# Batch 1's x in two groups of 48 rows, its stage A in side-by-side products, and the last evacuation of stage D a step later

## Chip, core and metric

The kernel runs on one core of one Trainium2 chip. The metric is the device time of one execution in microseconds (us), the median of several runs. Inputs are drawn once and are the same for all kernels.

## What is computed

A two-dimensional Fourier transform of x (8 batches of 3072 rows of 256 numbers), of which the real part is kept, and on its result a channel mix: each row is blended with the row before it, multiplied by weights, squared behind a relu, multiplied again and gated.

```python
def _attn_ref(x):                       # x: (8, 3072, 256)
    X = np.fft.fft(x, axis=1)
    X = np.fft.fft(X, axis=2)
    return X.real.astype(np.float32)

def _moe_ref(x, mu_k, mu_r, w_k, w_v, w_r):
    x_prev = np.concatenate([np.zeros((B, 1, D)), x[:, :-1, :]], axis=1)
    xk = mu_k * x + (1.0 - mu_k) * x_prev
    xr = mu_r * x + (1.0 - mu_r) * x_prev
    k = np.maximum(xk @ w_k, 0.0)       # w_k: 256 x 1024
    v = k * k @ w_v                     # w_v: 1024 x 256
    r = 1.0 / (1.0 + np.exp(-(xr @ w_r)))
    return r * v
```

## The kernel before

**Two halves that overlap.** The transform of a batch runs in stages A, D and C, all of them products on TensorE with tables of sines, each followed by an evacuation from PSUM by ScalarE or VectorE. The channel mix of a batch runs in chunks of 512 rows, six to a batch: products with w_k (`k_piece`, L912), a relu on ScalarE (L922), a square on VectorE (L932), products with w_v (L953; in the first chunks L965), products with w_r (`r_item`, L939) with a sigmoid on ScalarE (L944), and the output's product r·v on VectorE (`v_out`, L975), which is then stored.

**Steps.** A loop over 192 steps and a few more gives the order. Step s does the quarter s % 4 of chunk s // 4's w_k products. Around them stands what a table of `at(step, ...)` and `event(step, ...)` puts there: first the items of kind "x" (`r_item`, stage A by `a_sum` and `a_item`, stage D by `d_item`, the turning product `turned`), then the w_v products, then the events, then the items of kind "w", which are VectorE's (`fold`, `butterfly`, `mix`, `diff`) and the loads, then the output products `v_out` (ahead of the "w" items where the step is listed in `OUT_FIRST`), and last the square. So batch b's transform is computed while batch b−1 is mixed. The order of instructions on each engine is pinned to the order in which the code issues them: an engine that waits holds up all that is queued behind it.

**Batch 1 around steps 8 to 18.** x arrives by GpSimd's queue in two halves h, each as a forward part `xp` (`load_p`, a plain transfer, L138 or L135) and a mirrored part `xm` (`load_m`, a gather by row numbers, L141). `fold` (L172, L174) adds the two into `p`. In batches 0 and 1 the data lie on 96 partitions, one row number each. From batch 2 on they lie on 112 partitions, in two groups of 48 at partitions 0 and 64, each transferred by itself. Stage A of batch 1's half h = 0 is `a_sum` at steps 11 and 12 (L681): 8 products of 96 rows and 208 columns each. It takes `p` as it is. Half h = 1 is `a_item` at steps 13 and 14 (L594, L591): 7 products of 104 columns and 2 of 52 each, on `eo`, which `butterfly` (L211) makes of `p`. The other way of stage A, `a_half` (L663) with `a_slots_0` (L653), is used for batch 2: 48-row products of 52 columns, those of the rows 0 to 47 and those of the rows 64 to 111 in turn, into different PSUM banks. Its tables `w_h` and `w_h0` are made by `half_tables` at step 3 (L535).

Stage D is four `d_item`s (L703): two at step 15, two at step 16, evacuated by ScalarE and VectorE in turn. `turned` at step 17 (L752) then multiplies one column of all 13 units with a table, evacuated by ScalarE. Stage C (`c_pairs`, L803) begins at step 18.

**PSUM.** `ps_w` hands out three buffers of two banks in turn, `ps_v` two of one bank. A product into a buffer waits until the buffer's last contents were read.

## Time and profile before

| | us |
|---|---|
| median of 3 runs | 425.98 |
| lowest and highest | 425.94, 426.00 |
| the profiled execution's own time | 426.17 |
| its span in the profile | 424.4 |
| TensorE busy | 418.4 (99%) |
| VectorE busy | 371.3 (87%) |
| ScalarE busy | 332.4 (78%) |
| GpSimd busy | 64.2 (15%) |

The profile is of one execution. Engines: PE is TensorE's matmuls, PEld its weight loads, DVE VectorE, ACT ScalarE, POOL GpSimd, SP SyncE. L912 is line 912 of the kernel. A row of a timeline gives the start and the time in us, the engine, the line, the operation, the tiles (written <- read), the shape, and the count of merged instructions; in brackets stands an idle time before it and what ended it. A row of the windows gives the stretch, its length, the busy time of PE, PEld, DVE, ACT and POOL with the number of instructions, the granted clock, the share of the transfer engines and GB/s. The granted clock of TensorE is 1.00 throughout the profiled span. Times in the texts below are counted from the span's start.

### The profile page before, as it was taken

The numbers are of one execution on the slowest core, as the hardware profiler recorded it, in microseconds if no ns is written. First come the engines' busy times: TensorE is split into PE (matmuls) and PEld (weight loads), VectorE is DVE, ScalarE is ACT, GpSimd is POOL, SyncE is SP. The second block draws the span as 40 slices with busy tenths as digits, with TensorE's granted clock in tenths as the row PEclk, the third lists the DMA queues.
The fourth block names the chain that finished last, engine by engine and source line by source line (L and its number), as shares of the span: only waits on it lengthen the run. The fifth ranks groups of instructions, "written<-read, shape, count | busy, mean of one in ns | idle before, by whom it ended". The sixth has DMA issues, their size and how long they took to land.

```text
span 424.4 us, 9646 instructions
## 1 busy us (share of the span) xinstructions
PE 418.4 (99%) x3974; PEld 294.1 (69%) x3974; DVE 371.3 (87%) x593; ACT 332.4 (78%) x438; POOL 64.2 (15%) x99
## 2 busy tenths in 40 slices
PE   8999999999999999999999999999999999999996
PEld 3767766776677767776767776777777776776765
DVE  8899999999898999989999899989999676977553
ACT  7889886798768986699767996689876997666661
POOL 7478500200060001400041000500000000000000
PEclk9999999999999999999999999999999999999999
DMA  8779962632385223932349232772233232332333
GB/s 171 111 111 195 224 156 57 113 91 64 70 151 147 64 59 62 215 101 51 76 77 220 52 75 59 134 174 55 52 76 72 58 73 52 74 74 51 76 76 99
DMA packets 35104, 42.08 MB, mean 99 GB/s; under 512 B 4114, under 2 KB 31092, under 8 KB 35060
## 3 DMA queue, kind: packets, MB, share of 16 engines
q1 hardware_dynamic: 27488, 25.41, 24.4%
q0 software_dynamic: 7264, 15.80, 21.8%
q8 instruction: 31, 0.51, 0.5%
q10 hardware_dynamic: 308, 0.26, 0.2%
q14 instruction: 13, 0.11, 0.1%
HBM read 32.08 MB, written 25.17 MB: 135 GB/s over the span
## 4 chain that ended last, share of the span: by engine, by line
PE 98%; DVE 1%; issue 0%; POOL 0%; ACT 0%; POOLq 0%
PE psW L912 39%; PE psV L953 37%; PE psW L939 10%; PE psV L965 3%; PE psW L611 3%; PE psW L235 1%; PE psV L611 1%; PE psW L681 1%; PE psW L703 1%; PE psV L378 1%; PE psW L771 0%; PE psW L803 0%; DVE rw L308 0%; PE psV L703 0%; PE psW L663 0%
## 5 line engine op out<-in xcount | busy, mean ns | idle before, releaser
L922 ACT ACTIVATE rl<-psW 128x1024 f16<-128x1024 f32 x192 | 194.3, 1039 | 79.2 <-PE psW L912 75.5
L912 PE MATMUL psW<-x,wk 128*128 128x512 f16 (+1 forms) x776 | 194.4, 377 | 0.3 <-DVE x L1049 0.3
L953 PE MATMUL psV<-wv_sb,k 128*128 128x256 f16 x1424 | 184.2, 273 | 0.0
L953 PEld LDWEIGHTS <-k 128*128 128x128 f16 x1424 | 136.8, 98 | 38.9
L932 DVE TENSOR_TENSOR k<-rl 128x2048 f16<-128x2048 f16 (+1 forms) x100 | 115.5, 1156 | 32.9 <-ACT rl L922 32.8
L912 PEld LDWEIGHTS <-wk 128*128 128x128 f16 x776 | 75.7, 98 | 53.7 <-issue 0.4
L975 DVE SCALAR_TENSOR_TENSOR o<-psV,r 128x512 f32<-128x512 f32 (+1 forms) x97 | 65.7, 680 | 10.0 <-PE psV L953 9.0
L877 DVE TENSOR_TENSOR x<-y,t 128x1536 f16<-128x1536 f16 (+3 forms) x76 | 62.4, 827 | 2.2
L944 ACT ACTIVATE r<-psW 128x1024 f16<-128x1024 f32 x48 | 50.0, 1043 | 0.8 <-PE psW L939 0.8
L939 PE MATMUL psW<-wr,x 128*128 128x256 f16 x384 | 49.8, 273 | 0.0
L939 PEld LDWEIGHTS <-x 128*128 128x128 f16 x384 | 37.5, 98 | 14.1
L574 ACT ACTIVATE a<-psW 128x832 f16<-128x832 f32 (+4 forms) x36 | 29.0, 851 | 0.2 <-PE psW L663 0.2
L574 ACT ACTIVATE g_all<-psW 128x512 f16<-128x512 f32 (+5 forms) x47 | 26.7, 646 | 0.3 <-PE psW L703 0.2
L494 POOL IOTA gate<- 1x1 int32 x7 | 0.8, 121 | 163.4 <-DVE gate L493 163.4
L141 POOL DMA_INDIRECT xm<-in_x_dram,idx_g x18 | 23.3, 1294 | 5.5 <-issue 5.5
L866 DVE TENSOR_SCALAR t<-d,muf_t 128x1536 f16<-128x1536 f16 (+3 forms) x44 | 21.9, 508 | 0.1
L172 DVE TENSOR_TENSOR p<-xp,xm 112x2304 f16<-112x2304 f16 (+6 forms) x19 | 21.6, 1139 | 0.0
L574 ACT ACTIVATE pq<-psW 128x1024 f16<-128x1024 f32 (+1 forms) x21 | 20.4, 1007 | 0.1
L866 DVE TENSOR_SCALAR t<-d,mu_m 128x1536 f16<-128x1536 f16 x32 | 19.6, 611 | 0.0
L854 DVE TENSOR_TENSOR d<-y 128x1664 f16<-128x1664 f16 (+5 forms) x19 | 16.7, 879 | 0.3 <-ACT y L574 0.3
L846 DVE TENSOR_TENSOR y<-pq 128x960 f16<-128x960 f16 (+3 forms) x28 | 15.7, 603 | 0.4
L965 PE MATMUL psV<-wv_sb,k 128*128 128x256 f16 x112 | 14.7, 273 | 0.0
(158 smaller groups left out, 236.3 us busy)
## 6 DMA issues: line engine op xcount, KB each, us to landing
out_dram<-o SPq DMA_DIRECT2D x189, 128.0 KB, 2.4
xp<-in_x_dram POOLq DMA_DIRECT2D x12, 216.0 KB, 5.2
xp<-in_x_dram POOLq DMA_DIRECT2D x13, 192.0 KB, 6.8
xp<-in_x_dram POOLq DMA_DIRECT2D x2, 384.0 KB
wv_sb<-in_moe_w_v_dram POOLq DMA_DIRECT2D x1, 512.0 KB
xp<-in_x_dram SPq DMA_DIRECT2D x1, 480.0 KB, 4.3
xp<-in_x_dram POOLq DMA_DIRECT2D x1, 432.0 KB, 4.9
xm<-in_x_dram,idx_g POOLq DMA_INDIRECT x18, 6.9
```

The source lines that it names most:

```text
L141: nc.gpsimd.indirect_dma_start(dst, None, src, bass.IndirectOffsetOnAxis(ap=idx, axis=0))
L574: nc.scalar.activation(out=out_ap, in_=in_ap, func=AF.Copy)
L866: V.tensor_scalar(out=dst, in0=src, scalar1=mu, scalar2=None, op0=ALU.mult)
L877: V.tensor_tensor(out=_v(x_t[b, j, m], o, [(64 * step, hi - lo), (step, 64)]), in0=y_t[b][:, lo + 3 * m:hi + 3 * m, a], in1=x_t["t", a][:, ...
L912: nc.tensor.matmul(out=st["k", ds][:, 512 * hs + lo:512 * hs + hi], lhsT=wk_sb[m][a][:, 128 * fc:128 * fc + 128], rhs=xk[:, a, 512 * i + l ...
L922: nc.scalar.activation(out=st["rl"][:, 2 * ds:2 * ds + 2], in_=st["k", ds].rearrange("p (f t) -> p f t", f=2), func=AF.Relu, bias=0.0, sca ...
L932: V.tensor_tensor(out=k2_t[c][:, lo:hi], in0=r, in1=r, op=ALU.mult)
L939: nc.tensor.matmul(out=ps[:, 256 * tb:256 * tb + 256], lhsT=x_t[b, 1, m][:, a, 512 * i + 128 * tb: 512 * i + 128 * tb + 128], rhs=wr_sb[m] ...
L944: nc.scalar.activation(out=st["r", c], in_=ps, func=AF.Sigmoid)
L953: nc.tensor.matmul(out=st["v", tb - h][:, 256 * h:256 * h + 256], lhsT=k2_t[c][:, fc, 128 * tb:128 * tb + 128], rhs=wv_sb[:, fc], start=(f ...
L965: nc.tensor.matmul(out=st["v", tb - h][:, 256 * h:256 * h + 256], lhsT=k2_t[c][:, fc, 128 * tb:128 * tb + 128], rhs=wv_sb[:, fc], start=fc ...
L975: V.scalar_tensor_tensor(out=o.rearrange("p a b -> p (a b)")[:, 0:256 * n], in0=st["v", t0][:, 0:256 * n], scalar=16.0, in1=st["r", c][:, ...
```

## The change

- Batch 1's x is loaded and folded on 112 partitions in two groups, as batches 2 and up were. The first group's forward transfer now brings 64 rows instead of 48 in batches 1 to 3, so that the rows between the groups hold numbers; the two memsets that cleared them (`zero_rows`) are gone. The row numbers for the mirrored gathers are made earlier, before step 0.
- Stage A of batch 1, half h = 0: `a_sums`, two at step 11, each 16 products of 48 rows and 104 columns, row groups in turn, two products accumulated into one place. Their tables widen `w_hh` from 104 to 208 columns: `half_tables` does 7 products instead of 3.
- Stage A of batch 1, half h = 1: `a_slots_0` and two `a_half` at step 13, as in batch 2, instead of the two `a_item`. Both halves now stand as events behind the w_v products of their step.
- `OUT_FIRST` lists step 10: its two output products stand ahead of that step's mix part.
- The last `d_item` of batch 1 moves from step 16 to 17, and `turned` writes into that item's PSUM buffer behind its data instead of taking a new one.

```diff
     def parts(b):
-        return 112 if b > 1 else 96
+        return 112 if b else 96
...
-        if b > 1:
+        if b:
             for g in range(2):
+                k = 64 if g == 0 and b < 4 else N1
                 src = dataclasses.replace(x[b, 32 * g + r:32 * g + r + 1, :],
-                                          ap=[[64 * D, N1], [D, n], [1, D]])
-                nc.gpsimd.dma_start(out=xp_t[b, h][64 * g:64 * g + N1, 0:n], in_=src)
+                                          ap=[[64 * D, k], [D, n], [1, D]])
+                nc.gpsimd.dma_start(out=xp_t[b, h][64 * g:64 * g + k, 0:n], in_=src)
             return
...
-    w_hh = const.tile([112, 2 * WB], FP16)
-    w_h, w_h0 = w_hh[:, 0:WB], w_hh[:, WB:2 * WB]
+    w_hh = const.tile([112, 4 * WB], FP16)
+    w_h, w_h0 = w_hh[:, 0:WB], w_hh[:, 3 * WB:4 * WB]
...
+    def a_sums(b, h, i0):
+
+        if (h, i0) == (0, 0):
+            a_tile(b)
+        ps = ps_w()
+        for i in range(4):
+            for k in range(2):
+                for g in range(2):
+                    rows = slice(64 * g, 64 * g + N1)
+                    nc.tensor.matmul(out=_v(ps, 512 * g + 2 * WB * i, [(1, 2 * WB)]),
+                                     lhsT=p_t[b, h][rows, i0 + i + 1 - h, 128 * k:128 * k + 128],
+                                     rhs=_v(w_hh[rows], WB * k, [(1, 2 * WB)]),
+                                     start=(k == 0), stop=(k == 1))
+        evac(_v(a_t[b], 8 * h + i0, [(16, 2), (32, 2 * WB), (1, 4)]),
+             _v(ps, 0, [(512, 2), (1, 2 * WB), (2 * WB, 4)]), "A")
...
+    g_t = {}
+
     def d_item(b, n, eng="A"):
...
         ps = ps_w()
+        g_t[b] = ps
...
+    def turned_behind(b):
+        turned(0, 13, g_t[b][:, 512:525])
...
-    OUT_FIRST = (12, 20, 28, 36, 38, 40, *(24 * t - 48 + k for t in range(3, B) for k in (28, 32, 36)))
+    OUT_FIRST = (10, 12, 20, 28, 36, 38, 40, *(24 * t - 48 + k for t in range(3, B) for k in (28, 32, 36)))
...
-    at(11, a_sum, 1, 0, 0)
+    event(11, (a_sums, 1, 0, 0), (a_sums, 1, 0, 4))
     at(11, fold, 1, 1)
-    at(12, a_sum, 1, 0, 4)
...
-    at(13, a_item, 1, 1, 0)
+    event(13, (a_slots_0, 1), (a_half, 1, 1, 0), (a_half, 1, 1, 1))
...
-    at(14, a_item, 1, 1, 1)
...
-    at(16, d_item, 1, 3, "V")
+    at(17, d_item, 1, 3, "V")
     at(17, r_item, (0, 1, 0))
-    at(17, turned, 0, 13)
+    at(17, turned_behind, 1)
```

How the order changes on VectorE at step 10. L866 and L877 (after: L868 and L879) are the mix part, L975 (L977) the output products, L932 (L934) the square, L172 (L173) the fold of batch 1's second half. Before:

```order
L866 TENSOR_SCALAR t_743<-d,muf_t 128x512
L866 TENSOR_SCALAR t_745<-d,muf_t 128x512
L877 TENSOR_TENSOR x_503<-y,t_743 128x512
L877 TENSOR_TENSOR x_503<-y,t_745 128x512
L975 SCALAR_TENSOR_TENSOR o<-psV_652,r 128x512
L975 SCALAR_TENSOR_TENSOR o<-psV_657,r 128x512
L932 TENSOR_TENSOR k_670<-rl 128x1024
L172 TENSOR_TENSOR p_88<-xp_84,xm_79 96x2048
```

Now:

```order
L977 SCALAR_TENSOR_TENSOR o<-psV_656,r 128x512
L977 SCALAR_TENSOR_TENSOR o<-psV_661,r 128x512
L868 TENSOR_SCALAR t_755<-d,muf_t 128x512
L868 TENSOR_SCALAR t_757<-d,muf_t 128x512
L879 TENSOR_TENSOR x_509<-y,t_755 128x512
L879 TENSOR_TENSOR x_509<-y,t_757 128x512
L934 TENSOR_TENSOR k_674<-rl 128x1024
L173 TENSOR_TENSOR p_88<-xp_84,xm_79 112x2048
```

The two output products moved ahead of the four instructions of the mix part; square and fold stay behind both.

VectorE at steps 15 to 17. The two L572 are the evacuations of stage D's second and last item, L172 (L173) and L174 (L175) the fold of batch 2's first half, L211 (L212) its butterfly. Before:

```order
L932 TENSOR_TENSOR k_788<-rl 128x1024
L572 CAST g_all<-psW_919 128x2x8x64
L932 TENSOR_TENSOR k_788<-rl 128x1024
L572 CAST g_all<-psW_953 128x2x2x64
L172 TENSOR_TENSOR p_87<-xp_82,xm_80 112x2304
L174 TENSOR_TENSOR p_87<-xp_82,xm_80 112x9
L211 TENSOR_TENSOR eo<-p_87 112x9x128 x2
```

Now:

```order
L934 TENSOR_TENSOR k_818<-rl 128x1024
L572 CAST g_all<-psW_953 128x2x8x64
L934 TENSOR_TENSOR k_818<-rl 128x1024
L173 TENSOR_TENSOR p_87<-xp_82,xm_80 112x2304
L175 TENSOR_TENSOR p_87<-xp_82,xm_80 112x9
L572 CAST g_all<-psW_1003 128x2x2x64
L212 TENSOR_TENSOR eo<-p_87 112x9x128 x2
```

The fold of batch 2 moved ahead of the last evacuation.

GpSimd behind its second gate, where it issues batch 1's loads. L138 and L136 are the forward transfers, L141 and L142 the gathers, L508 to L511 the row numbers. Before:

```order
L138 DMA xp_83<-in_x_dram 96x2304
L141 DMA xm_81<-in_x_dram,idx_92 96x256
L141 DMA xm_81<-in_x_dram,idx_91 96x2048
L508 IOTA idx_g_93 64x16
L510 IOTA idx_g_94 64x8
L508 IOTA idx_g_93 48x16
L510 IOTA idx_g_94 48x8
L511 IOTA idx_g_94 1x8
L141 DMA wk_97<-in_moe_w_k_dram,row_i 128x1024
L141 DMA wk_98<-in_moe_w_k_dram,row_i 128x1024
L138 DMA xp_84<-in_x_dram 96x2048
L141 DMA xm_79<-in_x_dram,idx_91 96x2048
```

Now:

```order
L136 DMA xp_83<-in_x_dram 64x2304
L136 DMA xp_83<-in_x_dram 48x2304
L142 DMA xm_81<-in_x_dram,idx_g_94 112x256
L142 DMA xm_81<-in_x_dram,idx_g_93 112x2048
L142 DMA wk_97<-in_moe_w_k_dram,row_i 128x1024
L142 DMA wk_98<-in_moe_w_k_dram,row_i 128x1024
L136 DMA xp_84<-in_x_dram 64x2048
L136 DMA xp_84<-in_x_dram 48x2048
L142 DMA xm_79<-in_x_dram,idx_g_93 112x2048
```

The row numbers went ahead, the forward transfer became two, and all mirrored rows are 112 instead of 96.

More of the change, by code (lines that the diff above doesn't have):

```diff
@@ L150, in load_m0 @@
         else:
[L151 removed]
+            load_m(b, 0, 2048, 1, idx_g0[:, b:b + 1])
     def load_xh(b, h):
@@ L533, in half_tables @@
         turned(8, 13, ps, "")
-        for o, w, step in ((512, 0, 2), (512, 1, 2), (512 + WB, WA, 1)):
-            nc.tensor.matmul(out=ps[0:112, o:o + WB], lhsT=order[0:96, 0:112],
-                             rhs=_v(w_pm[0:96], w, [(step, WB)]), start=w != 1, stop=w > 0)
+        neg = 2 * (WA + WB)
+        for o, w, step, n in ((0, 0, 2, 2), (1, 0, 2, 2), (2, neg, 2, 2), (3, WA, 1, 1)):
+            for k in range(n):
+                nc.tensor.matmul(out=ps[0:112, 512 + WB * o:512 + WB * o + WB],
+                                 lhsT=order[0:96, 0:112],
+                                 rhs=_v(w_pm[0:96], w + k, [(step, WB)]),
+                                 start=k == 0, stop=k == n - 1)
         evac(_v(g_all, 256 * 8 + 128, [(256, 5)]), ps[:, 0:5], "A")
-        V.tensor_copy(out=w_hh, in_=ps[0:112, 512:512 + 2 * WB])
+        V.tensor_copy(out=w_hh, in_=ps[0:112, 512:512 + 4 * WB])
     w_d = const.tile([P, 2, 64], FP16)
```

37 lines of the change are left out of this document (8 added, 29 removed).

## Prediction

> **What bounds the kernel now.** I read the page's busy times and its chain of waits first.
>
> ```profile
> PE 418.4 (99%) x3974; PEld 294.1 (69%) x3974; DVE 371.3 (87%) x593; ACT 332.4 (78%) x438; POOL 64.2 (15%) x99
> ...
> PE 98%; DVE 1%; issue 0%; POOL 0%; ACT 0%; POOLq 0%
> ```
>
> TensorE (PE) works 99% of the span and makes 98% of the chain that ends last. Whatever shortens TensorE's row of work ends the kernel earlier, as long as nothing else then makes TensorE wait. So the second view is the windows by stage, at steps 10 and 11, where the change begins.
>
> ```profile
> 38.00:40.00 2.00, 2.00 (x18) 1.47 (x17) 2.00 (x6) 2.00 (x3) 1.71 (x3) 1.00 1.07 225
> ```
>
> TensorE, the first busy time, is busy 2.00 of 2.00 us, but VectorE (DVE), the third, 2.00 as well. VectorE has no reserve here; it only happens not to be waited for. The last column, GB/s, shows 225: the transfers are dense too. A gain on TensorE in this stretch must be tested against the other two.
>
> **The change part by part: TensorE.** The timeline of TensorE, columns start, time, engine, line, operation, count. Since the ends of matmuls are modelled, I use distances between starts.
>
> ```profile
> 39.33 0.88 PE L681 MATMUL psW<-w_pm,p 96*128 96x208 f16 x8
> 40.04 1.04 PE L965 MATMUL psV<-wv_sb,k 128*128 128x256 f16 x8
> 40.92 1.03 PE L912 MATMUL psW<-x,wk 128*128 128x512 f16 x4
> 41.78 0.88 PE L681 MATMUL psW<-w_pm,p 96*128 96x208 f16 x8
> 42.49 1.04 PE L965 MATMUL psV<-wv_sb,k 128*128 128x256 f16 x8
> ...
> 45.11 0.49 PE L594 MATMUL psW<-w_pm,eo 96*128 96x104 f16 x7
> 45.43 0.26 PE L591 MATMUL psW<-w_pm,eo 96*128 96x52 f16 x2
> 45.50 1.05 PE L965 MATMUL psV<-wv_sb,k 128*128 128x256 f16 x8
> ...
> 47.26 0.49 PE L594 MATMUL psW<-w_pm,eo 96*128 96x104 f16 x7
> ...
> 47.65 1.05 PE L965 MATMUL psV<-wv_sb,k 128*128 128x256 f16 x8
> ...
> 54.77 0.18 PE L752 MATMUL psW<-g_all,turn 128*128 128x13 f16 x1
> ```
>
> Batch 1's stage A takes 0.71 us (39.33 to 40.04) and again 0.71 (41.78 to 42.49) for the first half, 0.39 (45.11 to 45.50) and 0.39 (47.26 to 47.65) for the second: 2.20 us. What the new products cost is shown by products that already stand side by side, and the table's products by their own row.
>
> ```profile
> 23.42 0.31 PE L535 MATMUL psW<-w_pm,order 96*112 96x52 f16 x3
> 23.58 1.02 PE L912 MATMUL psW<-x,wk 128*128 128x512 f16 x4
> 24.44 1.04 PE L965 MATMUL psV<-wv_sb,k 128*128 128x256 f16 x8
> 25.41 0.62 PE L771 MATMUL psW<-m_cs,g_all 64*128 64x128 f16 x16
> 25.96 1.04 PE L912 MATMUL psW<-x,wk 128*128 128x512 f16 x4
> ...
> 82.75 0.22 PE L653 MATMUL psW<-w_hh,eo 112*128 112x52 f16 x2
> 82.89 0.78 PE L663 MATMUL psW<-w_hh,eo 48*128 48x52 f16 x46
> 83.60 1.05 PE L953 MATMUL psV<-wv_sb,k 128*128 128x256 f16 x8
> ```
>
> Sixteen products of 128 columns, on the two halves of the rows in turn (L771), take 0.55 us (25.41 to 25.96): 0.069 a pair. Forty-six of 52 columns (L663) take 0.71 (82.89 to 83.60): 0.031 a pair. The new first half is 16 pairs of 104 columns. Between the two rows by columns a pair is 0.031 + 0.038 × 52/76 = 0.057, so 0.91 us. Entering this form costs 0.1: the eight products at 24.44 take 0.97 until the next group, where the eight at 40.04 take 0.88. Together 1.01 against 1.42, **−0.41**; with the prices of the two rows as bounds −0.82 and −0.22. The second half is two products for slot 0 (0.14, from 82.75 to 82.89) and 15 pairs of 52 columns (0.47): 0.61 against 0.78, **−0.17**. The tables at step 3 get four more products at 0.16/3 each (23.42 to 23.58): **+0.21**. Nothing hides these; TensorE has no gap there. The two last products of stage D and the turning product move but stay as many. Net on TensorE: **−0.37** (−0.78 to −0.18).
>
> The four evacuations of stage A stay four, of the same size, on ScalarE (ACT). Can they hold TensorE back?
>
> ```profile
> 41.98 1.02 ACT L922 ACTIVATE rl<-psW 128x1024 f16<-128x1024 f32 x1 [0.55 <-PE psW L912]
> ```
>
> ScalarE stands 0.55 us idle between two of them, waiting for TensorE's next product, so they cannot: I keep −0.37. The Trainium skill, TensorEngine Tiling (Array Packing), section Performance Considerations, says that packing speeds up TensorE but not the emptying of PSUM, which may then become the limit. By that rule stage A would gain nothing, and the sum on TensorE would be the tables' +0.21 alone; the idle 0.55 us do not agree with it for ScalarE.
>
> **The change on VectorE.** The two output products of step 10 (L975) now stand ahead of the last mix part instead of behind it. When can they start?
>
> ```profile
> 29.77 1.04 PE L965 MATMUL psV<-wv_sb,k 128*128 128x256 f16 x8
> ...
> 37.59 1.04 PE L965 MATMUL psV<-wv_sb,k 128*128 128x256 f16 x8
> ...
> 30.48 1.29 DVE L975 SCALAR_TENSOR_TENSOR o<-psV,r 128x512 f32<-128x512 f32 x2 [0.51 <-PE psV L965]
> ```
>
> At step 6 L975 stood idle 0.51 us for TensorE and started 0.71 after its products began (29.77 to 30.48). For step 10 that is 37.59 + 0.21 (tables) + 0.71 = 38.51. All times of VectorE from 30.48 on carry the 0.21 as well, for it was waiting for TensorE there.
>
> ```profile
> 37.87 0.66 DVE L866 TENSOR_SCALAR t<-d,muf_t 128x512 f16<-128x512 f16 x2
> ...
> 39.12 1.28 DVE L975 SCALAR_TENSOR_TENSOR o<-psV,r 128x512 f32<-128x512 f32 x2
> 40.32 0.67 DVE L932 TENSOR_TENSOR k<-rl 128x1024 f16<-128x1024 f16 x1
> 41.03 1.22 DVE L172 TENSOR_TENSOR p<-xp,xm 96x2048 f16<-96x2048 f16 x1
> ...
> 48.44 1.28 DVE L975 SCALAR_TENSOR_TENSOR o<-psV,r 128x512 f32<-128x512 f32 x2
> 49.63 0.68 DVE L932 TENSOR_TENSOR k<-rl 128x1024 f16<-128x1024 f16 x1
> 50.50 1.22 DVE L572 CAST g_all<-psW 128x1024 f16<-128x1024 f32 x1 [0.19 <-PE psW L703]
> 51.64 0.68 DVE L932 TENSOR_TENSOR k<-rl 128x1024 f16<-128x1024 f16 x1
> 52.36 0.42 DVE L572 CAST g_all<-psW 128x256 f16<-128x256 f32 x1
> 52.70 1.35 DVE L172 TENSOR_TENSOR p<-xp,xm 112x2304 f16<-112x2304 f16 x1
> ...
> 54.32 1.43 DVE L211 TENSOR_TENSOR eo<-p 112x1152 f16<-112x1152 f16 x2
> ```
>
> VectorE comes to this place at 37.87 + 0.21 = 38.08, so it now **stands 0.43 us**, where before it did the mix part. Then L975 twice (1.20, from 39.12 to 40.32), the mix part (1.25, from 37.87 to 39.12) and the square (0.71, to 41.03): the fold of batch 1's second half starts at 41.67, not 41.03. From there 7.41 us of work without a gap lead to L975 of step 14 (48.44), now at 49.08. That is why the cover of the 0.43 is gone: between steps 10 and 14 VectorE had no other idle time to give. Next come L975 twice (1.19) and a square. Where nothing is waited for, a row starts 0.08 before the last one's end (50.50 + 1.22 and 51.64), so a square of 0.68 takes 0.60: the evacuation of stage D's second item starts at 50.87, the next square 1.14 later at 52.01, the fold of batch 2 at 52.61. **This fold now stands ahead of stage D's last evacuation**, and fold to successor takes 1.62 (52.70 to 54.32). So the evacuation starts at 54.23 and ends at 54.65. The turning product needs it. TensorE came to that product at 54.77 before and could come now at 54.40; it must wait for VectorE until about 54.70, some hundredths of handover included. Queued behind it on TensorE are the output products, the next step's products and stage C. What TensorE won goes to a wait: 54.70 against 54.77, **−0.07**. The wider copy of the tables (208 columns for 104) lies before an idle moment of VectorE and costs nothing.
>
> **The change in the transfers.** Batch 1's first load carries 16 more rows in each piece: 72 KB for x forward, 8 and 64 for x mirrored, and for the second half 64 and 64, together 272 KB, before the fold at 41.67 can run. GpSimd issues two transfers more but five iotas and two memsets less in this place, about even.
>
> ```profile
> 29.95 0.95 POOL L141 DMA_INDIRECT wk<-in_moe_w_k_dram,row_i  x1 [0.30 <-issue]
> ...
> wk<-in_moe_w_k_dram,row_i POOLq DMA_INDIRECT x1, 6.6
> ...
> out_dram<-o SPq DMA_DIRECT2D x3, 128.0 KB, 9.2
> ```
>
> The second weight gather is issued at 29.95 and lands 6.6 later, 36.55. Behind it on its queue are two times 384 KB for batch 1's second half. At 225 GB/s that is 3.5 us: they land at about 40.0, and in any case by 41.03, when the fold starts without a wait. The added 272 KB take 1.2 us: **41.3 to 42.3**, nearest to the middle of the two, and a little later since step 10's stores go out 0.6 earlier. I take 42.0: VectorE waits 0.33 at the fold, and since everything from there to 54.70 is without a gap, TensorE ends 0.33 later: **+0.33** (0 to +0.6). The loads of batch 2 are 72 and 64 KB larger as well; their fold comes eleven us later and has more room.
>
> **The sum.** −0.07 + 0.33 = +0.26 on the profiled execution's 426.17 us (a span of 424.4 and what lies around it), 426.4. The median of the runs, 425.98, lies 0.19 below it, so **426.2 us**.
>
> **The rivals.**
>
> *TensorE's gain comes through.* If VectorE makes up its 0.43, or the order of the two at step 17 does not bind, the end is −0.37: 425.6, at best −0.78, 425.2. For it: the chain is TensorE's to 98%, and no wait for VectorE is in the rows above. Against it: VectorE's 2.00 of 2.00.
>
> *The load comes later still: slower.* One mechanism: the transfer for batch 1's second half lands after VectorE wants it, VectorE stands at the fold, and each us of that reaches the turning product. It costs from a landing at about 41.7 on, and more than 0.2% from 42.6. For it: the stores issued in the stretch 31 to 33 took 9.2 us to land (the last row above), so stores and loads hold each other up. Step 10's stores are 4 × 128 KB, 2.3 us at 225 GB/s; if half of that comes before the last packets, the landing is 43.0 and the end 43.0 − 41.67 − 0.07, +1.26: 427.2. Against it: these stores were issued before the load's end in the old order too. DMA: Bandwidth & Descriptors of the Trainium skill, section Queues, rings and completion order, has each DMA engine take its queues in turn, packet by packet, which is this sharing; the 9.2 us agree with it, and by that rule this rival is the likelier.
>
> *The products do not run side by side.* The pairs then cost two singles. Seven single products of 104 columns take 0.32 (45.11 to 45.43), 0.046 each: 32 × 0.046 + 0.1 for the first half is +0.15, 30 × 0.046 + 0.14 for the second at most +0.74, and with the tables TensorE is up to 1.1 longer: 427.1. Against it stand both rows of pairs; only the accumulation of two products into one place, with 48 rows, is not shown there at 104 columns.
>
> **How the numbers follow.** My forecast 0.5, TensorE's gain 0.25, the late load 0.2, no overlap 0.05. What a measurement of this kernel can tell from no change is taken as 0.2%, 0.85 us: under 425.13 is faster, over 426.83 slower. The forecast and nearly all of the first rival lie within, so the same gets 0.74. Faster, 0.05, is the first rival's far end, with something I do not see. Slower, 0.21, is the late load, part of the last rival and the forecast's upper tail. The range goes from the middle of the first rival's bounds, 425.4, to just short of the late load's 427.2, 427.1.
>
> **What would show it.** Right: stage A's first half takes 1.0 us and the second 0.6; L975 of step 10 has an idle of about 0.4 before it, by TensorE; TensorE's turning product of step 17 waits for VectorE's evacuation; VectorE's fold at about 42 waits for the load. Wrong: no idle before that turning product (then the first rival), pairs above 0.07 (the last), or an idle of over 1 us before the fold. A wait anywhere before step 10 or after step 20 that was not there before would overturn the sum, since I take these as unchanged.

## The result, and the profile after

The changed kernel took 427.09 us (median of ten runs, 426.81 to 428.27), the kernel before 426.21 (ten runs, 425.91 to 426.67). The ratio is 1.0023, with a 95% interval of 1.0013 to 1.0033: slower by about 0.23%, a small loss, but one that the interval sets apart from no change. The profiled execution took 426.86 us with a span of 425.1, against 426.17 and 424.4. Of all that follows, four executions at a lower granted clock or far off the others are left out: 544 to 623 us (three, the kernel before) and 1838 us (e13_both_behind).

The page of the changed kernel, busy times and chain of waits:

```profile
PE 417.9 (98%) x4008; PEld 292.8 (69%) x4008; DVE 371.7 (87%) x593; ACT 332.4 (78%) x438; POOL 63.2 (15%) x99
...
PE 90%; DVE 6%; DMA 2%; issue 1%; POOL 1%; ACT 0%; DVEq 0%; POOLq 0%
```

TensorE works 0.5 us less than before, and yet the end comes later: its share of the chain fell from 98% to 90%. 6% are now VectorE's and 2% a transfer's. Where that is, TensorE's timeline shows.

```profile
23.30 0.17 PE L754 MATMUL psW<-g_all,turn 128*128 128x5 f16 x1
23.32 0.52 PE L533 MATMUL psW<-w_pm,order 96*112 96x52 f16 x7
23.69 1.02 PE L914 MATMUL psW<-x,wk 128*128 128x512 f16 x4
24.55 1.04 PE L967 MATMUL psV<-wv_sb,k 128*128 128x256 f16 x8
...
38.57 1.03 PE L914 MATMUL psW<-x,wk 128*128 128x512 f16 x4
39.67 1.20 PE L967 MATMUL psV<-wv_sb,k 128*128 128x256 f16 x8
40.80 0.91 PE L658 MATMUL psW<-w_hh,p 48*128 48x104 f16 x32
41.64 1.04 PE L914 MATMUL psW<-x,wk 128*128 128x512 f16 x4
...
45.99 0.21 PE L633 MATMUL psW<-w_hh,eo 112*128 112x52 f16 x2
46.14 0.57 PE L643 MATMUL psW<-w_hh,eo 48*128 48x52 f16 x30
46.65 1.04 PE L914 MATMUL psW<-x,wk 128*128 128x512 f16 x4
...
49.26 1.06 PE L699 MATMUL psW<-w_eo,a 128*128 128x128 f16 x16
50.65 0.60 PE L967 MATMUL psV<-wv_sb,k 128*128 128x256 f16 x4 [0.33 <-DVE o L977]
...
54.24 1.04 PE L941 MATMUL psW<-wr,x 128*128 128x256 f16 x8
55.39 0.18 PE L754 MATMUL psW<-g_all,turn 128*128 128x13 f16 x1
...
56.81 0.64 PE L805 MATMUL psW<-m_cs,g_all 64*128 64x64 f16 x32
```

By starts: the tables take 0.37 (23.32 to 23.69), stage A's first half 0.84 (40.80 to 41.64), its second 0.66 (45.99 to 46.65). Before, these were 0.16, 1.42 and 0.78, so TensorE gains on balance. The waits, which the bracket shows at only one place, are read as starts that come late. The w_k products at 38.57 take 1.10 to the next start, where at 23.69 they take 0.86: a wait of 0.24. The eight at 39.67 take 1.13, where in e1_early below they take 0.97: 0.16. From stage D's sixteen to the next start it is 1.39, where the kernel before took 0.89: 0.50. The w_r products at 54.24 take 1.15 for 0.87: 0.28. Together 1.18 us. All four are read as waits for VectorE: the first three for a PSUM buffer that it empties (at 50.65 the bracket names its output products, and at 39.67 the chain of waits has them directly ahead), the last for stage D's evacuation. VectorE's timeline in the changed kernel:

```profile
30.59 1.29 DVE L977 SCALAR_TENSOR_TENSOR o<-psV,r 128x512 f32<-128x512 f32 x2 [0.51 <-PE psV L967]
...
34.04 1.36 DVE L173 TENSOR_TENSOR p<-xp,xm 112x2304 f16<-112x2304 f16 x1 [0.56 <-DMA xm<-in_x_dram,idx_g]
...
38.93 1.28 DVE L977 SCALAR_TENSOR_TENSOR o<-psV,r 128x512 f32<-128x512 f32 x2
...
42.50 1.23 DVE L173 TENSOR_TENSOR p<-xp,xm 112x2048 f16<-112x2048 f16 x1 [0.49 <-DMA xm<-in_x_dram,idx_g]
...
49.91 1.28 DVE L977 SCALAR_TENSOR_TENSOR o<-psV,r 128x512 f32<-128x512 f32 x2
...
53.44 1.35 DVE L173 TENSOR_TENSOR p<-xp,xm 112x2304 f16<-112x2304 f16 x1
54.83 0.20 DVE L175 TENSOR_TENSOR p<-xp,xm 112x9 f16<-112x9 f16 x1
54.92 0.42 DVE L572 CAST g_all<-psW 128x256 f16<-128x256 f32 x1
```

Both folds of batch 1 wait for their mirrored load (`xm`), 0.56 and 0.49 us. Between 42.50 and 54.92 VectorE has no gap, and its last evacuation ends at 55.34; TensorE's turning product starts at 55.39. In the kernel before neither fold waited. The first, on VectorE's timeline of that kernel, and on TensorE's the rows that answer to the first and the last one above:

```profile
33.08 1.35 DVE L172 TENSOR_TENSOR p<-xp,xm 96x2304 f16<-96x2304 f16 x1
```

```profile
23.39 0.17 PE L752 MATMUL psW<-g_all,turn 128*128 128x5 f16 x1
...
56.19 0.64 PE L803 MATMUL psW<-m_cs,g_all 64*128 64x64 f16 x32
```

Stage C starts at 56.81 against 56.19: 0.62 us later. From there to the end of the span both kernels take the same, 368.3 and 368.2 us. So the loss arises before stage C.

### The profile page after: what moved, and what is told of

The parts are those of the page before. It is cut to its first block, busy times and chain, and to the rows that moved or that the text cites. A ratio compares the mean times of both kernels' runs of the same rounds, so it can differ in the third digit from the quotient of the medians.

```text
span 425.1 us, 9716 instructions
## 1 busy us (share of the span) xinstructions
PE 417.9 (98%) x4008; PEld 292.8 (69%) x4008; DVE 371.7 (87%) x593; ACT 332.4 (78%) x438; POOL 63.2 (15%) x99
## 4 chain that ended last, share of the span: by engine, by line
PE 90%; DVE 6%; DMA 2%; issue 1%; POOL 1%; ACT 0%; DVEq 0%; POOLq 0%
PE psV L955 37%; PE psW L914 36%; PE psW L941 9%; PE psW L591 3%; DMA xm<-in_x_dram,idx_g 2%; PE psV L967 1%; DVE p L173 1%; PE psV L591 1%; DVE rl L309 1%; PE psW L699 1%; PE psW L677 1%; DVE x L879 1%; DVE t L868 1%; DVE g_all L572 0%; DVE k L934 0%
## 5 line engine op out<-in xcount | busy, mean ns | idle before, releaser
L955 PE MATMUL psV<-wv_sb,k 128*128 128x256 f16 x1424 | 184.2, 273 | 0.0
L934 DVE TENSOR_TENSOR k<-rl 128x2048 f16<-128x2048 f16 (+1 forms) x100 | 115.6, 1157 | 32.8 <-ACT rl L924 32.6
L977 DVE SCALAR_TENSOR_TENSOR o<-psV,r 128x512 f32<-128x512 f32 (+1 forms) x97 | 65.8, 681 | 9.8 <-PE psV L955 8.9
L879 DVE TENSOR_TENSOR x<-y,t 128x1536 f16<-128x1536 f16 (+3 forms) x76 | 62.4, 827 | 2.2
L142 POOL DMA_INDIRECT xm<-in_x_dram,idx_g x21 | 26.2, 1249 | 6.8 <-issue 6.1
L173 DVE TENSOR_TENSOR p<-xp,xm 112x2304 f16<-112x2304 f16 (+4 forms) x19 | 21.7, 1141 | 1.1 <-DMA xm<-in_x_dram,idx_g 1.1
L868 DVE TENSOR_SCALAR t<-d,muf_t 128x1536 f16<-128x1536 f16 (+3 forms) x44 | 22.1, 513 | 0.1
L868 DVE TENSOR_SCALAR t<-d,mu_m 128x1536 f16<-128x1536 f16 x32 | 19.6, 613 | 0.0
L136 POOL DMA_DIRECT2D xp<-in_x_dram x28 | 15.7, 572 | 1.7 <-DMA xm<-in_x_dram,idx_g 0.8
```

The source lines that it names most:

```text
L142: nc.gpsimd.indirect_dma_start(dst, None, src, bass.IndirectOffsetOnAxis(ap=idx, axis=0))
L173: V.tensor_tensor(out=p[:, q0:q0 + n], in0=xp[:, q0:q0 + n], in1=_v(xm, o + 256, [(-256, n), (-1, 256)]), op=ALU.add)
L868: V.tensor_scalar(out=dst, in0=src, scalar1=mu, scalar2=None, op0=ALU.mult)
L879: V.tensor_tensor(out=_v(x_t[b, j, m], o, [(64 * step, hi - lo), (step, 64)]), in0=y_t[b][:, lo + 3 * m:hi + 3 * m, a], in1=x_t["t", a][:, ...
L934: V.tensor_tensor(out=k2_t[c][:, lo:hi], in0=r, in1=r, op=ALU.mult)
L955: nc.tensor.matmul(out=st["v", tb - h][:, 256 * h:256 * h + 256], lhsT=k2_t[c][:, fc, 128 * tb:128 * tb + 128], rhs=wv_sb[:, fc], start=(f ...
```

## The experiments

The start of an execution varies by itself (last section). So each profiled run is also measured by the **stretch** from step 3's turning product (five columns) to stage C's first group (x32): 32.80 us in the kernel before (23.39 to 56.19), 33.51 in the changed one (23.30 to 56.81). Theories: **L**, the late loads are the loss; **O**, the new order on VectorE is (output products ahead, evacuation behind the fold); **P**, the products themselves cost more; **S**, transfers moved early disturb the start. The experiments ran on four chips; each ratio is to runs of the kernel before on the same chip, whose medians were 426.10 (e1 to e4), 426.44 (e5 to e8), 426.48 (e9 to e11, after_again) and 426.52 (e12 to e14). It is estimated from all runs and is not the quotient of the two medians.

| run | median us (low to high) | ratio to the kernel before, 95% | waits of the two folds | step 3's turning product | stretch |
|---|---|---|---|---|---|
| changed kernel | 427.09 (426.81–428.27) | 1.0023 [1.0013, 1.0033] | 0.56, 0.49 | 23.30 | 33.51 |
| after_again | 428.00 (427.45–428.94) | 1.0038 [1.0023, 1.0052] | 1.13, 0.78 | 23.30 | 34.15 |
| e1_early | 426.97 (425.81–427.70) | 1.0015 [1.0004, 1.0026] | none | 23.53 | 32.48 |
| e2_bytes | 426.74 (425.91–428.05) | 1.0006 [0.9996, 1.0015] | 0, 1.19 | 24.69 | 33.55 |
| e3_d16 | 427.59 (427.03–428.38) | 1.0038 [1.0024, 1.0052] | 0.44, 0.28 | 23.51 | 33.48 |
| e4_out10 | 427.43 (426.64–429.89) | 1.0035 [1.0022, 1.0049] | 0, 0.76 | 23.33 | 33.33 |
| e8_evac | 428.78 (428.41–429.39) | 1.0059 [1.0046, 1.0072] | 0.67, 0.57 | 23.73 | 33.26 |
| e5_gate0 | 427.49 (427.03–429.10) | 1.0033 [1.0019, 1.0046] | none | 23.99 | 33.00 |
| e7_gate0_evac | 429.26 (428.37–429.96) | 1.0061 [1.0048, 1.0073] | none | 25.90 | 32.35 |
| e6_before_gate0 | 427.12 (426.76–428.66) | 1.0020 [1.0011, 1.0029] | none | 25.86 | 32.81 |
| e9_nogate1 | 427.06 (426.64–427.30) | 1.0011 [1.0002, 1.0020] | none | 23.76 | 33.36 |
| e10_wk_later | 427.09 (425.86–428.34) | 1.0015 [1.0003, 1.0027] | none | 23.30 | 32.60 |
| e11_both | 426.46 (426.00–426.56) | 0.9995 [0.9986, 1.0004] | none | 23.75 | 32.75 |
| e12_gate_behind | 426.91 (426.77–427.93) | 1.0017 [1.0008, 1.0025] | none | 23.30 | 33.54 |
| e13_both_behind | 426.77 (426.30–427.41) | 1.0007 [0.9998, 1.0016] | none | 23.79 | 32.95 |
| e14_before_both | 426.49 (425.98–426.65) | 0.9998 [0.9989, 1.0007] | none | 23.78 | 32.80 |

The last three columns are of the one profiled execution, read from timelines as above; a wait of under 0.15 us counts as none.

### Are the loads the loss?

**e1_early**: in the changed kernel batch 1's first-half load is issued at the end of the first loads, without the wait that held it back, some 8 us earlier (15.36 against 23.31).

```diff
     def loads():
...
+        load_xh(1, 0)
...
     def loads_1():
         load_gate()
-        load_xh(1, 0)
```

> Edit: the changed kernel, with batch 1's first-half load issued some 7 us earlier, right behind the row numbers, without its gate. Theory L (late loads: VectorE's two waits for batch 1's x, 0.56 and 0.49 us, carry the loss): both idles before the folds of batch 1 vanish, an idle of about 0.4 for TensorE appears before the output products of step 10, and the time comes to 426.0 to 426.3, within 0.2 of the kernel before. Theory O (order on VectorE: output products first at step 10, batch 2's fold ahead of the last evacuation): the loss stays, +0.6 to +0.9. Theory P (the side-by-side products and the longer tables cost more than they save): the loss stays as well.

The timelines of VectorE and of TensorE:

```profile
38.64 1.29 DVE L977 SCALAR_TENSOR_TENSOR o<-psV,r 128x512 f32<-128x512 f32 x2 [0.27 <-PE psV L967]
...
41.65 1.22 DVE L173 TENSOR_TENSOR p<-xp,xm 112x2048 f16<-112x2048 f16 x1
```

```profile
53.59 1.04 PE L941 MATMUL psW<-wr,x 128*128 128x256 f16 x8
54.59 0.18 PE L754 MATMUL psW<-g_all,turn 128*128 128x13 f16 x1
...
56.01 0.64 PE L805 MATMUL psW<-m_cs,g_all 64*128 64x64 f16 x32
```

With no load late, the output products of step 10 stand idle for TensorE (0.27), as the prediction had it for the changed kernel, and the stretch falls to 32.48, 1.03 under the changed kernel and 0.32 under the kernel before. The second fold tells where this comes from: it starts 18.12 us after step 3's turning product (41.65 − 23.53), in the changed kernel 19.20 (42.50 − 23.30), 1.08 later. That is the whole difference: theory L. That the two waits add up to about as much, 1.05, is chance: the first fold starts 0.77 later than here (0.56 of waiting, the rest a mix part ahead of it that took longer), but at the output products of step 10 only 0.52 of that is left, for VectorE has idle time there. The run times do not keep the gain. The median of 426.97 missed the expected 426.0 to 426.3: three of eleven came at 425.8 to 426.0, the others at 426.7 to 427.7. The profiled execution was one of the three; what held the others up is not known.

**e2_bytes**: the kernel before with only batch 1's transfers widened to 112 rows. The 16 rows more are loaded and never read.

```diff
-        nc.gpsimd.dma_start(out=xp_t[b, h][0:96, q0:q0 + n], in_=src)
+        k = 112 if b else 96
+        nc.gpsimd.dma_start(out=xp_t[b, h][0:k, q0:q0 + n], in_=src)
```

> Edit: the kernel before, with the loads of batch 1 on 112 rows instead of 96 and nothing else (16 more rows are brought and not used). Theory L: idles of 0.3 to 0.6 us before the folds of batch 1, and the time is +0.3 to +0.9 over the kernel before. Theories O and P: no change, within 0.1.

VectorE's second fold and TensorE's stage C:

```profile
43.48 1.22 DVE L173 TENSOR_TENSOR p<-xp,xm 96x2048 f16<-96x2048 f16 x1 [1.19 <-DMA xm<-in_x_dram,idx]
```

```profile
58.24 0.64 PE L804 MATMUL psW<-m_cs,g_all 64*128 64x64 f16 x32
```

The bytes alone make the second fold wait, and the stretch grows by 0.75, with the old products and the old order. The mirrored gather of that fold is issued 8.39 us after step 3's turning product, as in the kernel before; here it lands 10.3 us after its issue, while there the fold ran 9.25 us after the issue without a wait. The first fold does not wait, though theory L expected it to. Over the runs the ratio (1.0006) is not told from no change; the profiled execution was the longest of eleven. That a load of this size can come this late is shown; how often is not.

### Are the other parts?

**e3_d16** puts the last `d_item` back to step 16 and gives the turning product its own PSUM buffer; **e4_out10** takes step 10 out of `OUT_FIRST`; **e8_evac** moves the fold of batch 2 behind that last evacuation.

```diff
-    at(17, d_item, 1, 3, "V")
+    at(16, d_item, 1, 3, "V")
...
-    at(17, turned_behind, 1)
+    at(17, turned, 0, 13)
```

```diff
-    OUT_FIRST = (10, 12, 20, 28, 36, 38, 40, *(24 * t - 48 + k for t in range(3, B) for k in (28, 32, 36)))
+    OUT_FIRST = (12, 20, 28, 36, 38, 40, *(24 * t - 48 + k for t in range(3, B) for k in (28, 32, 36)))
```

```diff
-    at(16, fold, 2, 0)
+    at(17, fold, 2, 0)
```

> Edit: the changed kernel, with stage D's last item back at step 16 and the turning product in a PSUM buffer of its own, as before. Theory L: the wait before the turning product (0.28 us) goes, the two waits at the folds stay; +0.4 to +0.7 over the kernel before. Theory O: most of the loss goes, within 0.2 of the kernel before. Theory P: no change against the changed kernel.

> Edit: the changed kernel, with the output products of step 10 behind the mix part again. Theory L: TensorE waits over 1 us more at step 11 for the PSUM buffers, but the second fold waits for its load anyway, so from there on VectorE is as before and the end is within 0.3 of the changed kernel. Theory O: 0.4 faster than the changed kernel, since VectorE loses no time before the output products. Theory P: no change.

> Edit: the changed kernel, with batch 2's first fold moved to step 17, behind stage D's last evacuation. Theory L: the wait of 0.28 us before the turning product goes, the waits at the folds stay; stage C begins 33.2 to 33.3 us after step 3's turning product; time 0.2 to 0.3 under the changed kernel. Theory O: most of the loss goes, to within 0.2 of the kernel before.

TensorE's timeline of e3_d16 and of e4_out10, then VectorE's and TensorE's of e8_evac:

```profile
52.85 0.27 PE L699 MATMUL psW<-w_eo,a 128*128 128x128 f16 x2 [0.42 <-DVE g_all L572]
```

```profile
40.28 1.20 PE L967 MATMUL psV<-wv_sb,k 128*128 128x256 f16 x8 [0.65 <-DVE o L977]
```

```profile
54.90 0.42 DVE L572 CAST g_all<-psW 128x256 f16<-128x256 f32 x1 [0.92 <-PE psW L699]
```

```profile
60.61 1.02 PE L914 MATMUL psW<-x,wk 128*128 128x512 f16 x4 [1.13 <-DVE pq L572]
```

Each undo only moves TensorE's wait: to the last item of stage D (0.42), to step 11's buffers (0.65), or behind stage C (1.13), where the next products wait for VectorE, which then has the fold of batch 2 in front. With e8_evac VectorE stands 0.92 us idle at the evacuation and lacks them later. The last of these waits lies behind the stretch; e8_evac, expected 0.2 to 0.3 under the changed kernel, came out longer than it, 428.78. The stretch stays at 33.3 to 33.5 while the second fold waits; in e4_out10, as in e2_bytes, the first one does not, and the loss is there. That theory O is not the loss is shown best by e1_early, which has all of the new order and a stretch under that of the kernel before. Nor is it P: stage A of batch 1 took 1.60 us (0.84, 0.66 and 0.10 for going over to the side-by-side products), predicted were 1.62.

### Can the load simply go earlier?

**e5_gate0**: the load is issued at the first gate, 2.6 us earlier, with w_r's gathers ungated ahead of it. **e7_gate0_evac** adds the edit of e8_evac. **e6_before_gate0** is the kernel before with the edit of e5_gate0.

```diff
     def loads():
...
+        for a in range(2):
+            gather(wr_sb[0][a], moe_w_r, row_i[:, a:a + 1])
...
     def loads_0():
         load_gate()
-        for a in range(2):
-            gather(wr_sb[0][a], moe_w_r, row_i[:, a:a + 1])
+        load_xh(1, 0)
...
     def loads_1():
         load_gate()
-        load_xh(1, 0)
```

> Edit: the changed kernel, with batch 1's first-half load moved to the first gate (about 3 us earlier), and the first two w_r gathers ahead of that gate. Theory L: no wait for the load at either fold, stage C of step 18 begins 32.5 us after step 3's turning product (32.8 in the kernel before, 33.5 in the changed one), and the time is 425.7 to 426.1. Theory S (early transfers delay the start: the load issued before step 0 in the first trial made most executions 0.9 longer): the first step begins later in most executions, and the median stays at 426.7 or above. Theory O: as the changed kernel, 427.0.

> Edit: as the kernel with the load at the first gate, and batch 2's first fold moved from step 16 to step 17, so that stage D's last evacuation stands ahead of it on VectorE. Theory L with VectorE as the bound of what is left: the turning product waits no longer (0.13 in the first trial), and stage C begins 32.2 to 32.4 us after step 3's turning product; time 425.5 to 425.9. Without that wait as a cause: the same as the load at the first gate, within 0.1.

> Edit: the kernel before, with the load of batch 1's first half at the first gate and the first two w_r gathers ahead of it, 96 rows as before. Theory L: nothing to win, since no fold waited there; stage C begins 32.8 us after step 3's turning product and the time is within 0.15 of the kernel before. Theory S: if early transfers cost at the start, it shows here too, +0.5 to +0.9 in the median.

TensorE in e6_before_gate0:

```profile
17.04 0.23 PE L771 MATMUL psW<-m_cs,g 64*128 64x128 f16 x1 [0.59 <-DVE g L308]
...
19.30 1.54 PE L912 MATMUL psW<-x,wk 128*128 128x256 f16 x8 [0.36 <-DVE x L1049]
...
21.48 1.83 PE L912 MATMUL psW<-x,wk 128*128 128x256 f16 x8
```

The stretch is 32.81 here: nothing to win where no fold waits, as theory L says. But the runs are 0.2% slower: the early transfers cost in the kernel before too, which speaks for theory S. In the profiled execution step 3 stands at 25.86, 2.5 us late; it was the longest of the eleven (428.66), and the median is only 0.7 us up, so that the loss of the others lies at the start is likely and not shown. In e5_gate0 no fold waits either, but step 3 at 23.99, 0.7 late, eats the 0.5 that the stretch gives: 427.49, as theory S expected, and not the 425.7 to 426.1 of theory L. e7_gate0_evac has the expected stretch (32.35) but missed its 425.5 to 425.9 by far: step 3 stands at 25.90, and the wait behind stage C of e8_evac is there too.

### The load less than a microsecond earlier, and less ahead of it

**e9_nogate1** drops the gate at step 1, so that the load follows w_r's gathers at once; **e10_wk_later** puts the second half's load ahead of w_k's second gathers (the second diff); **e11_both** does both; **after_again** is the changed kernel on the same chip as these three.

```diff
     def loads_1():
-        load_gate()
         load_xh(1, 0)
```

```diff
     def loads_2():
+        load_xh(1, 1)
         for a in range(2):
             gather(wk_sb[1][a], moe_w_k, row_i[:, 2 + a:3 + a])
-        load_xh(1, 1)
```

> The changed kernel without the wait that holds batch 1's first-half load back until step 1 (the load is issued right behind w_r's gathers, some 0.6 us earlier, as that wait measured 0.52 in the changed kernel's trace; nothing before 23 us moves). Theory L (the two waits of the folds are the loss): the first fold's wait of 0.56 falls to 0 to 0.1, the second's of 0.49 to 0 to 0.3, some of the TensorE's gain still comes back as waits at PSUM buffers; from the 5-column turning product of step 3 to stage C's x32 in 32.7 to 33.1 (the changed kernel 33.51, the kernel before 32.80), and 426.0 to 426.5 in all. Theory O (the order on VectorE): 33.4 to 33.5 and 427.0, whatever the loads do. Theory S (an earlier load disturbs the start): none here, since the load does not pass the first gathers; a late start in this run would speak against S as a matter of the place before the gate.

> The changed kernel with batch 1's second-half load ahead of the second pair of w_k's gathers (two gathers less ahead of it, 2.2 us of GpSimd's issue time and their bytes). Theory L: the second fold's wait of 0.49 goes to 0, the first's of 0.56 stays; the end of the chain was late by both, so stage C's x32 stands 0.3 to 0.5 earlier than in the changed kernel: 33.0 to 33.2 after the step-3 turning product, 426.6 in all. If the first wait alone sets it: 33.5 as in the changed kernel. If w_k's second pair is now late, TensorE waits near 41 to 42 us at the 128x512 product whose weights it is.

> Both edits together. Theory L: neither fold waits, the VectorE's chain to the CAST of stage D's last item is as with the early load (32.5 to 32.7 from the step-3 turning product to stage C's x32), and with an undisturbed start 425.6 to 426.0, under the kernel before. Theory O: 33.4 to 33.5 and 427.0. If what is left is TensorE waiting on buffers and VectorE at 0.3 idle only, 32.8 and 426.2: no better than before.

> The changed kernel once more, on the chip of the three runs above: 427.1 as in its first runs (426.8 to 428.3), with 0.4 to 0.6 of wait at both folds and 33.4 to 33.6 from the step-3 turning product to stage C's x32. If it comes out at 426.3 or less, the chip or its day made the difference of the first runs.

VectorE's timeline in after_again, then in e11_both:

```profile
34.40 1.36 DVE L173 TENSOR_TENSOR p<-xp,xm 112x2304 f16<-112x2304 f16 x1 [1.13 <-DMA xm<-in_x_dram,idx_g]
...
43.15 1.23 DVE L173 TENSOR_TENSOR p<-xp,xm 112x2048 f16<-112x2048 f16 x1 [0.78 <-DMA xm<-in_x_dram,idx_g]
```

```profile
33.69 1.34 DVE L173 TENSOR_TENSOR p<-xp,xm 112x2304 f16<-112x2304 f16 x1
...
38.88 1.29 DVE L977 SCALAR_TENSOR_TENSOR o<-psV,r 128x512 f32<-128x512 f32 x2 [0.23 <-PE psV L967]
41.88 1.22 DVE L173 TENSOR_TENSOR p<-xp,xm 112x2048 f16<-112x2048 f16 x1
```

Two executions of the changed kernel that both have VectorE's output products of step 6 at 30.59 differ in the folds: in after_again the second starts 0.65 later (43.15 against 42.50), and the stretch is 0.64 longer (34.15 against 33.51). There GpSimd spent 1.74 us instead of 0.96 on issuing the weight gather ahead, so the load itself was issued 0.78 later. In all thirteen profiled runs of the changed kernel and its variants the second fold starts 18.1 to 19.9 us after step 3's turning product, and stage C 14.1 to 14.7 us after that fold: the start of the second fold sets the stretch to within some 0.6. With both moves no fold waits and the kernel is level with the one before: 426.46 against 426.48, no run over 426.56, where after_again has 428.00 on the same chip. The expectation of 425.6 to 426.0 missed. For e10_wk_later the expected 0.56 at the first fold was absent although that load was not moved, and its runs spread over 2.5 us: one move is not enough to be safe. e9_nogate1 came out as theory O had it (33.36 and 427.06); but neither of its folds waits, and the next runs show what does.

**e12_gate_behind** and **e13_both_behind** repeat e9_nogate1 and e11_both with the gate kept, behind the load, so that no engine but GpSimd has another row than in the changed kernel; **e14_before_both** is the kernel before with both moves.

```diff
     def loads_1():
-        load_gate()
         load_xh(1, 0)
+        load_gate()
```

> The changed kernel with the wait of step 1 put behind batch 1's first-half load instead of ahead of it: every engine but GpSimd issues exactly what it issues in the changed kernel, and the load starts 0.5 to 0.6 us earlier, as in the run without that wait. Rival A (the 0.46 by which the step-3 turning product stood later without the wait, 23.76 against 23.30, comes from the two instructions that were missing there): 23.3 here. Rival B (it differs from one execution to the next): anywhere from 23.3 to 23.8 here. Theory L: the first fold's wait 0 to 0.1, the second's 0 to 0.5, 32.7 to 33.2 from the step-3 turning product to stage C's x32, 426.3 to 426.9 in all by rival A. Should TensorE wait again near 28 us for the ScalarE's copy of y, as without the wait (0.58), the earlier load itself disturbs that copy: then 33.3 and 427.0.

> The same with batch 1's second-half load ahead of the second pair of w_k's gathers as well. Theory L: no fold waits, VectorE idles 0.2 to 0.3 for TensorE at step 10 as the prediction had it, 32.4 to 32.8 from the step-3 turning product to stage C's x32; with the start at 23.3 stage C at 55.7 to 56.1, 425.6 to 426.1 in all, 0.0 to 0.6 under the kernel before. With the start at 23.75: 426.1 to 426.5, no better than the kernel before. Theory O: 427.0.

> The kernel before with the same two moves of its loads. Its folds do not wait, so theory L gives it nothing: 32.7 to 32.9 from the step-3 turning product to stage C's x32, 426.2 to 426.6, within 0.3 of the kernel before. What the changed kernel with the same moves is better than this, the products of stage A are worth with the loads out of the way: 0 to 0.4 by theory L (the rest of TensorE's gain is lost to the VectorE's chain). If this run too is faster by 0.3 or more, the moves of the loads are worth something by themselves.

The timelines of ScalarE and of TensorE in e12_gate_behind, then VectorE's in e13_both_behind:

```profile
27.61 1.02 ACT L574 ACTIVATE y<-psW 128x1024 f16<-128x1024 f32 x1 [1.83 <-PE psW L914]
```

```profile
28.68 0.29 PE L773 MATMUL psW<-m_cs,g_all 64*128 64x128 f16 x4 [0.70 <-ACT y L574]
```

```profile
39.09 1.29 DVE L977 SCALAR_TENSOR_TENSOR o<-psV,r 128x512 f32<-128x512 f32 x2 [0.33 <-PE psV L967]
```

The earlier load removes the folds' waits, but ScalarE stands 1.83 us idle ahead of its copy of y, where in the changed kernel it stands 0.41, and TensorE waits 0.70 at 28.68: 33.54, nothing won. The long idle came with the load's move in each of these runs (1.71 in e9_nogate1, 1.03 and 1.10 with both moves, 0.77 in e14_before_both) and in e5_gate0 (1.29), but not in e1_early, e6_before_gate0 and e7_gate0_evac (0.41 each), whose load moved by 2 us or more, as that of e5_gate0 did. So it is no matter of an earlier load alone, and its cause stays open. The kernel before with both moves is unchanged (0.9998; stretch 32.80). The changed kernel with both has 32.75 and 32.95, and its runs, 426.46 and 426.77, are longer than theory L expected: the late copy takes back what the loads give. Only e1_early and e10_wk_later, where that copy is hardly late (0.41 and 0.52), show the products' gain in the stretch (32.48 and 32.60), in one execution each. In the run times no version here beats the kernel before.

## Why the prediction was wrong

It forecast 426.2, +0.2 on the 425.98 of the kernel before, and no measurable change; measured are +0.88 on 426.21, and the kernel is slower. 427.09 lies just inside the range, whose upper end is 427.1. Of the 0.9 us above the forecast 0.23 is the kernel before, whose ten runs have a higher median than its first three. Stage C accounts for 0.36 (56.81, forecast 56.19 + 0.26). Another 0.23 is what the median lies above the profiled execution, and no trace shows it.

**TensorE, −0.37.** Right. The tables cost +0.21 as said. The first half took 0.84, and going over to the side-by-side form 0.10, which shows in e1_early, where nothing waits there (VectorE is ahead): its eight v products of step 11 take 0.97 to the next start, for 0.88 before (39.67 to 40.64, the next rows). The second half took 0.66, with 0.61 predicted. Net 0.21 − (1.42 − 0.94) − (0.78 − 0.66) = −0.39.

```profile
39.67 1.04 PE L967 MATMUL psV<-wv_sb,k 128*128 128x256 f16 x8
40.64 0.91 PE L658 MATMUL psW<-w_hh,p 48*128 48x104 f16 x32
```

**VectorE, −0.07: the mechanism right, the size off by up to 0.25.** The evacuation behind batch 2's fold ended at 55.34 and the turning product, which waited for it, started at 55.39, a handover of 0.05. With the loads out of the way the change measures −0.32 (e1_early) and −0.20 (e10_wk_later), where ScalarE's copy is late as well −0.05 and +0.15 (e11_both, e13_both_behind). So in e1_early most of what TensorE gains comes through, and only 0.13 us of it (53.59 to 54.59, 1.00 for 0.87) goes to this wait. Two steps of the term were too long: from the output products of step 10 to the fold it took 3.16, and e1_early shows 3.01. And from the fold to its successor it took 1.62, from a row whose successor reads the fold's result; the evacuation does not, and followed in 1.48 (53.44 to 54.92).

**The transfers, +0.33: the step that failed, in its size.** The mechanism came true: VectorE waits at the second fold for its load, and the wait reaches the turning product. But the load was taken to land at 42.0, between 41.3 and 42.3, and the fold could start only at 42.50, 10.8 us after the mirrored gather's issue at 31.69. Against the 41.67 at which the prediction has VectorE come to this fold that is 0.83, not 0.33. With 0.83, and with the 1.48 above for 1.62, its chain gives 54.65 + 0.83 − 0.14 = 55.34 for the end of the last evacuation, which is what was measured. Against e1_early, where no load is late, the second fold costs 1.08: −0.32 + 1.08 = +0.76, and the stretch grew by 0.71. e1_early takes this away, and e2_bytes, the kernel before with the wider loads alone, puts 0.75 in.

The prediction also gave the first half's load no term, with GpSimd's issues "about even". For the second half they were (31.69 against 31.78). For the first they were not, since the iotas that fell out stand behind its load: its last gather was issued 0.88 later. On GpSimd's timeline and in the issues to landing, first the kernel before, then the changed one:

```profile
25.70 1.97 POOL L141 DMA_INDIRECT xm<-in_x_dram,idx  x1 [0.30 <-issue]
...
xm<-in_x_dram,idx POOLq DMA_INDIRECT x1, 6.0
```

```profile
26.58 1.13 POOL L142 DMA_INDIRECT xm<-in_x_dram,idx_g  x1 [0.30 <-issue]
31.69 1.00 POOL L142 DMA_INDIRECT xm<-in_x_dram,idx_g  x1 [0.30 <-issue]
...
xm<-in_x_dram,idx_g POOLq DMA_INDIRECT x1, 7.3
```

Before, this gather landed at 31.7, 1.4 us ahead of its fold at 33.08; in the changed kernel at 33.9, and the fold waited 0.56. By these rows that wait did not lengthen the changed kernel: VectorE came to the second fold at 42.01 and stood there 0.49 more. It did take away the idle of 0.43 at step 10.

The 9.2 us of the stores in the kernel before pointed at a later landing. The Trainium skill, DMA: Bandwidth & Descriptors, section Queues, rings and completion order, has each DMA engine take its queues in turn, which goes the same way. No run here separates that from mere bytes.

**The rivals.** "The load comes later still" is what happened in its sign and its mechanism. It had the landing at 43.0, measured are 42.50; that its 427.2 is so near to 427.09 is in part chance, by the 0.23 above. Its 0.2 was too little. The trace of before shows the 1.4 us of reserve for the first half's load, but no landing for the second's. "TensorE's gain comes through" fell for the kernel as it is; without the late loads it holds for the most part in e1_early's stretch (−0.32 of −0.39), and in no run times. "The products do not run side by side" fell: a pair of 104 columns took 0.84/16 = 0.052.

**PSUM.** The rule of the Trainium skill, TensorEngine Tiling (Array Packing), section Performance Considerations, that packing does not speed the emptying of PSUM, was weighed for stage A's evacuations, and these did not bind. TensorE does wait at 50.65 and, in after_again and e4_out10, at step 11 for buffers of the channel mix that VectorE empties. But in e1_early, where no load is late, these waits are absent (stage D's sixteen products take 0.89 to the next start, as before the change), so the trace shows no such limit by the faster products here.

## What to carry to other kernels

Where an engine has no idle time, ask of every load it will read how early it lands now: issue plus landing time, against the start of its reader. A load without a wait in the trace has a reserve that is not seen in the waits, and a kernel whose loads grow needs that reserve measured. A gain on the busiest engine is worth what the second-busiest leaves of it: here, with the loads late, 0.4 us of products came out as waits at PSUM buffers and at one evacuation. And where a load is moved to cure this, the runs have to show that no new wait arises: here six of the nine versions that issue the first half's load earlier had one, at a copy that does not read this load.

## What the runs showed that was not expected

- **The start has two places.** Step 3's turning product stands at 23.30 to 23.53 in eight profiled runs and at 23.73 to 23.79 in five (the other four are later); e13_both_behind, whose program is that of the changed kernel up to there, is of the second kind. There, on TensorE's timeline, a wait stands at 13.73 for a copy on ScalarE:

```profile
13.73 0.70 PE L677 MATMUL psV<-w_pm,p 96*128 96x208 f16 x6 [0.37 <-ACT muf_t L1010]
```

  The changed kernel has no such wait there. Some run times of the kernel before lie in two groups as well: on the chip of e9 to e11 seven lie at 425.97 to 426.10 and the others from 426.32 on. On the other chips the groups run into each other, and that the one explains the other was not tested.
- **Where transfers moved early, TensorE's own products were slower at the start of some executions.** In e6_before_gate0 eight w_k products took 1.33 and 1.66 to the next start, where the kernel before has 0.87 and 0.96, and the granted clock was 0.96 between 20 and 60 us (0.97 in e7_gate0_evac; 1.00 in the kernel before, the changed one, e5_gate0, e10_wk_later and e13_both_behind). Waits of TensorE alone do not explain it: between 10 and 20 us it was busy for 8.88 of 10 us in e6_before_gate0 and for 8.65 in e5_gate0. The cause stays open.
- **A copy on ScalarE came late in six of the nine versions that issue the first half's load earlier**, though it does not read that load (0.77 to 1.83 us idle ahead of it, 0.41 in the changed kernel). What it waited for is not in the trace: the products named as its releaser had ended.
